# Gated attention and GLU on one core: loads of remixed input moved to SyncE, pair loads two periods later, routing sums in halves of 256 columns

## The chip, the cores and the metric

The kernel runs on one core of a Trainium2 chip. The metric is the device time of one execution in microseconds (us): the median of the runs shown. The engines are TensorE (PE), VectorE (DVE), ScalarE (ACT), GpSimd (POOL) and SyncE (SP); SP only issues transfers.

## What is computed

For 2048 tokens `x` of 512 columns, a gate chooses per token between two branches, a full softmax attention with 32 heads of 16 columns and a GLU with 1792 hidden columns, all in fp32:

```python
g = sigmoid((x * gate_w).sum(-1, keepdims=True))
qkv = x @ wqkv                                   # 32 heads, 16 columns each
p = softmax(q @ k.T * 16 ** -0.5)
a = (p @ v) @ wo
b = (sigmoid(x @ w_gate) * (x @ w_up)) @ w_down
out = g * a + (1 - g) * b
```

The sum in the first line, one number a token, is called the routing sum or logit here.

## The kernel before, in words

Products in fp32 are made from pairs of tiles, a rounded high part and what is left (`xh`, `xl` for the input). The attention runs in 256 steps of the loop `for k in range(NPER)`, here called periods: two heads by two key tiles at a time. A period has these parts.

- The scores of tiles that come later, on PE (line 709), and their exponentials on ACT (line 711), eight of 512 columns, into the tiles `p`.
- The scores of rows whose maxima are needed later, on PE (line 298), and their reductions on DVE (lines 311, 316, 318), nine in a period. Line 311 does one score tile in two parts of 192 and 320 columns, and begins DVE's work of the period. The maxima of a whole half of a pair of heads go through `mpad` and a transpose, every eighth period, into two rows of the tile `qs`, so that the exponentials need no subtraction.
- Twelve matmuls of the GLU and of the late projections (line 164, `dn`), which a generator `filling()` hands out as jobs `far`, `side` and `chain`; when such a sum is complete, `leave` (line 632) copies it with ACT into one of six `er` tiles, and POOL adds such tiles (line 567).
- At the end the values phase: 32 matmuls (line 874) of `p` with `v`. ACT copies the result in two halves (line 882, `sum` in the first period of a group of eight, else `part`), and POOL adds the `part` tiles (line 892).

The string `STEADY` fixes the order of words in a period, and PE, ACT, DVE and POOL execute in the order of the program (`ORDERED`). Only the order of the transfers on SP is chosen by the framework's scheduler.

`load_pair` (lines 258, 259) brings the next pair of heads, eight transfers into `qs` and `ks`, once in sixteen periods; the maxima's scores read it five periods later, since they run `LEAD` = 22 steps, eleven periods, ahead. `mixed_x` (line 401) replaces parts of `xh` and `xl` by sums and differences of input parts kept in `t_d`, at the ends of some jobs, 28 transfers in all. Between `k` = 75 and 122, in groups of six periods, `logit_load` brings 256 tokens (`xn`) and `logits` (line 859) makes two routing sums on DVE; in the same groups the late projections are split (`split_load`, `split_sum`).

Of the kernel before, what the change touches and what calls it, by code (L numbers as in the profile page):

```python
# [12 lines left out]
F32 = mybir.dt.float32  # L13
F32R = mybir.dt.float32r
AF = mybir.ActivationFunctionType
ALU = mybir.AluOpType
# [6 lines left out]
SYNC = mybir.DependencyInfo(mybir.DependencyClass.Sync, mybir.DependencyReason.DATA)  # L23

S, D, H, DH, F = 2048, 512, 32, 16, 1792
# [5 lines left out]
NPAIR = H // 2  # L31
# [16 lines left out]
def gated_mix(ctx, tc, x, xT, wqk, wv, wo, w_gate, w_up, w_down, gate_w, out):  # L48
    nc = tc.nc
    pe, act, dve, pool, sp = nc.tensor, nc.scalar, nc.vector, nc.gpsimd, nc.sync  # L50
# [6 lines left out]
    def turns(tiles):  # L57
        turn = iter(range(1 << 30))
        return lambda: tiles[next(turn) % len(tiles)]
# [18 lines left out]
    t_d = dram.tile([5, 2, 2, 2, P, 512], F32, name="t_d")  # L78
# [12 lines left out]
    logit = keep.tile([P, NS], F32, name="logit")  # L91
    g1 = keep.tile([P, NS], F32, name="g1")
    g0 = keep.tile([P, NS], F32, name="g0")
# [4 lines left out]
    def mid(name, dt=F32):  # L98
        return keep.tile([P, 4, 512], dt, name=name, tag="mid", bufs=3)
# [107 lines left out]
    gwb = xp.tile([P, D], F32, name="gwb")  # L207
# [189 lines left out]
    def mixed_x(n, c, k0, cx):  # L397

        cols = slice(cx * 512, (cx + 1) * 512)
        for a, xs in enumerate((xh, xl)):  # L400
            act.dma_start(xs[:, k0:k0 + 2, cols].bitcast(F32), t_d[n, a, c].rearrange("k p s -> p k s"))

    def o_and_r(u, ks, ot, rb):

# [224 lines left out]
                    kept_x(4, c, 2, c + 2)  # L629
        wd.extend(ws)  # L630

    leave = lambda e, o: act.activation(e, o, AF.Copy)
    fill = filling()


# [9 lines left out]
    for c in range(NC):  # L645
# [20 lines left out]
        for i, m in order:  # L666
            o, ops, dst = two[i]
# [23 lines left out]
        else:  # L691
            engine.tensor_copy(to, o)

    ptile = {}

    def st_part(k, b):

        p, r = divmod(2 * k, 32)
        i, kt = divmod(r, 16)
        qs, ks = QS[p % 2], KS[p % 2]  # L700
        r = 64 * b
        pt = ptile[k, b] = mid(f"p{k}_{b}")

        def steps():
            for a in range(2):
                for c in range(2):
                    o = bank()
                    q0 = i * 1024 + c * 512
                    pe.matmul(o, ks[r:r + KR, (kt + a) * P:(kt + a + 1) * P], qs[r:r + KR, q0:q0 + 512],  # L709
                              start=True, stop=True)  # L710
                    act.activation(pt[:, 2 * a + c, :], o, AF.Exp, scale=DH ** -0.5)  # L711
                    yield
        return steps()

# [136 lines left out]
    tok = {}  # L851
# [2 lines left out]
        tok[t] = keep.tile([P, 2, D], F32, name=f"xn{t}", tag="ev", bufs=2)  # L854
        sp.dma_start(tok[t], x[t * P:(t + 2) * P, :].rearrange("(t p) d -> p t d", p=P))

    def logits(t, a):
        xn = tok[t][:, a, :]
        dve.tensor_tensor_reduce(xn, xn, gwb, scale=1.0, scalar=0.0, op0=ALU.mult, op1=ALU.add,
                                 accum_out=logit[:, t + a:t + a + 1])  # L860

    VALUES = (("18", 0), ("19", 256))
    sums = {}
# [74 lines left out]
    bank = bankm = lambda: spot[0]  # L938
    for k in range(NPER):
        n = 2 * k  # L940
        if n + LEAD == NSTEP:
            last = [before[s] for s in ("14", "12", "17", "15", "18", "16", "19")]
            bank = turns(last)
            leave = dve.tensor_copy
        if 75 <= k < 123:
            t, r = divmod(k - 75, 6)
            if r in (0, 3):
                split_load(2 * t + r // 3)
            if r in (1, 4):
                split_sum(2 * t + r // 3)  # L950
            if r == 1:
                logit_load(2 * t)
            if r in (3, 4):
                logits(2 * t, r - 3)
        if n % 32 == 0 and n // 32 + 1 < NPAIR:
            load_pair(n // 32 + 1)
        parts["t0"], parts["t1"] = st_part(k, 0), st_part(k + 1, 1) if k + 1 < NPER else iter(())
        emit(STEADY if k < FREE else LAST, **parts)
        if run and run.done():
            run = next(fill, None)  # L960
        elif run and run.n:
            turn(run)
        for half in list(mrow):
            later[:0] = put_max(half)
        work(2.6)
        later.extend(soon)
        soon.clear()
        if k == NPER - 1:
            break
        if NPER - 16 < k <= NPER - 12:  # L970
            for _ in range(2):
                next(next(exps))
        if k < FREE:
            slots.update({"18": slots["10"], "19": slots["13"]})
        values(k)
        before, slots = slots, {}
        if k == NPER - 17:
            loaded.extend(hidden_load(*chunks[m]) for m in range(2))
            early = [hidden_early(m) for m in range(2)]
            exps = iter([early[0]] * 4 + [early[1]] * 4)  # L980
        if 192 <= k < 215 and k % 8 != 4:
            next(dens[0], None)
        if k == NPER - 6:
            next(dens[1])
        if k == NPER - 2:
            raws = [late_raw(*late[m][:2]) for m in range(2)]
        if k == NPER - 13:
            early = chain(*early)
        if k >= NPER - 13:
            for _ in range(1 if k < FREE else 3):  # L990
                next(early, None)
# [71 lines left out]
    at = dict(zip((9, 11, 13, 15, 18, 20, 23, 25), range(8)))  # L1063
# [66 lines left out]
```

## Time and profile before

| what | us |
|---|---|
| median of three runs (lowest, highest) | 1676.27 (1675.6, 1678.23) |
| the profiled execution | 1674.28 |
| its span | 1672.5 |
| PE busy | 1663.9 |
| DVE busy | 1470.0 |
| ACT busy | 1403.3 |
| POOL busy | 942.2 |

The span runs from the first to the last instruction of the profile. Busy time is summed over the whole span, while each stage has its own limits; the attention loop fills the time from 88 to 1486 us. A bracket behind a row of a timeline tells how long the engine was idle ahead of it and which event ended that.

### The profile page before, as it was taken

Reading aid. Unit: us, or ns where it says so; the run is one execution under the profiler, and the core shown is the slowest. Engines: PE = TensorE matmul, PEld = TensorE weight load, DVE = VectorE, ACT = ScalarE, POOL = GpSimd, SP = SyncE. Lnnn points to the kernel's source line nnn. Section 1 sums busy time; section 2 is a strip of 40 time slices with the busy share of each in tenths; the row PEclk is TensorE's granted clock in tenths of the full one; section 3 lists DMA queues with packets and bytes.
Section 4 is the critical chain, followed back from the end, with each engine's and each line's share of the span. In section 5 each row is a group of like instructions: output and inputs, shape, how many; then the busy total and the mean of one; then the engine's idle time right before and its main releaser. Section 6 shows DMA issues by size and latency. Waiting matters only on the chain.

```text
span 1672.5 us, 43216 instructions
## 1 busy us (share of the span) xinstructions
PE 1663.9 (99%) x16650; PEld 1211.0 (72%) x16650; DVE 1470.0 (88%) x2595; ACT 1403.3 (84%) x2901; POOL 942.2 (56%) x922
## 2 busy tenths in 40 slices
PE   9999999999999999999999999999999999999999
PEld 7777777777677777676677777777777777668887
DVE  7989999999889999999899999999999999886853
ACT  4189999999999999998899999999999999983431
POOL 1134576547656666566667677676766667553110
PEclk9999999999999999999999999999999999999999
DMA  8412447365555565556535353534353435368861
GB/s 271 121 47 62 131 170 214 139 186 191 152 192 153 159 165 162 148 160 197 138 110 141 109 147 103 141 103 135 111 134 109 134 115 171 110 214 267 300 211 70
DMA packets 143822, 254.75 MB, mean 152 GB/s; under 512 B 24256, under 2 KB 36544, under 8 KB 140736
## 3 DMA queue, kind: packets, MB, share of 16 engines
q1 hardware_dynamic: 135024, 235.34, 46.3%
q10 hardware_dynamic: 8592, 16.65, 3.2%
q8 instruction: 131, 2.15, 0.6%
q14 instruction: 75, 0.61, 0.1%
HBM read 149.42 MB, written 102.50 MB: 151 GB/s over the span
## 4 chain that ended last, share of the span: by engine, by line
PE 99%; DMA 1%; POOL 0%; DVE 0%; ACTq 0%; ACT 0%; issue 0%; SPq 0%; POOLq 0%
PE sm L874 21%; PE dn L164 17%; PE sm L709 13%; PE sm L298 10%; PE st L298 9%; PE st L874 7%; PE st L709 7%; PE st L1075 3%; PE sm L1075 3%; PE dn L1075 2%; PE st L164 2%; PE st L669 1%; PE sm L151 1%; PE st L151 1%; DMA qs<-q_d 0%; DMA side_7r<-in_w_up_dram 0%
## 5 line engine op out<-in xcount | busy, mean ns | idle before, releaser
L711 ACT ACTIVATE p<-sm 128x512 f32<-128x512 f32 x1274 | 704.0, 631 | 20.6 <-PE sm L709 10.4
L316 DVE TENSOR_REDUCE stat<-sm 128x1 f32<-128x512 f32 x802 | 521.3, 681 | 0.3 <-PE dn L164 0.2
L709 PE MATMUL sm<-qs,ks 64*128 64x512 f32 x1274 | 497.6, 417 | 0.0
L316 DVE TENSOR_REDUCE stat<-st 128x1 f32<-128x512 f32 x734 | 479.6, 681 | 4.2 <-PE dn L164 4.2
L711 ACT ACTIVATE p<-st 128x512 f32<-128x512 f32 x774 | 462.1, 636 | 9.4 <-PE st L709 0.3
L298 PE MATMUL sm<-ks,qs 48*128 48x512 f32 (+2 forms) x1192 | 421.8, 391 | 0.0
L298 PE MATMUL st<-ks,qs 48*128 48x320 f32 x1101 | 394.6, 390 | 0.0
L874 PE MATMUL sm<-p,v 128*17 128x256 f32 (+1 forms) x6000 | 377.6, 384 | 0.0
L892 POOL TENSOR_TENSOR sum<-sum,part 128x512 f32<-128x512 f32 x224 | 288.2, 1287 | 133.5 <-PE sm L709 34.9
L709 PE MATMUL st<-qs,ks 64*128 64x512 f32 x774 | 318.1, 427 | 3.7 <-ACT part L882 3.7
L874 PEld LDWEIGHTS sm<-p,v 128*17 128x17 f32 x6000 | 164.3, 97 | 159.1 <-DVE stat L316 32.1
L298 PEld LDWEIGHTS sm<-ks,qs 48*128 48x128 f32 x1192 | 200.5, 186 | 71.7 <-ACT part L882 49.6
L709 PEld LDWEIGHTS sm<-qs,ks 64*128 64x128 f32 x1274 | 233.3, 185 | 25.8 <-issue 5.1
L298 PEld LDWEIGHTS st<-ks,qs 48*128 48x128 f32 x1101 | 188.6, 186 | 66.0 <-ACT part L882 37.3
L567 POOL TENSOR_TENSOR chain<-chain,chain 128x512 f32<-128x512 f32 x96 | 124.3, 1295 | 150.6 <-PE sm L709 54.9
L882 ACT ACTIVATE part<-sm 128x256 f32<-128x256 f32 x306 | 125.9, 413 | 55.6 <-PE sm L874 54.3
L709 PEld LDWEIGHTS st<-qs,ks 64*128 64x128 f32 x774 | 142.5, 185 | 21.1 <-ACT part L882 4.6
L311 DVE TENSOR_REDUCE stat<-sm 128x1 f32<-128x192 f32 x245 | 97.6, 419 | 59.6 <-PE sm L298 58.8
L567 POOL TENSOR_TENSOR had<-chain,had 128x512 f32<-128x512 f32 x96 | 123.5, 1286 | 39.2 <-PE sm L709 19.7
L311 DVE TENSOR_REDUCE stat<-st 128x1 f32<-128x320 f32 x245 | 97.7, 420 | 47.5 <-PE st L298 47.0
L874 PE MATMUL st<-p,v 128*17 128x256 f32 (+1 forms) x2016 | 136.8, 389 | 0.0
L318 DVE TENSOR_REDUCE stat<-sm 128x2 f32<-128x512 f32 x145 | 97.9, 682 | 0.0
(917 smaller groups left out, 3590.8 us busy)
## 6 DMA issues: line engine op xcount, KB each, us to landing
gul<-gu_d SPq DMA_DIRECT2D x56, 512.0 KB
had<-gu_d SPq DMA_DIRECT2D x84, 256.0 KB
gu_d<-had SPq DMA_DIRECT2D x84, 256.0 KB
gu_d<-side SPq DMA_DIRECT2D x56, 256.0 KB
pv_d<-sum SPq DMA_DIRECT2D x32, 256.0 KB
qs<-q_d SPq DMA_DIRECT2D x30, 256.0 KB
ks<-k_d SPq DMA_DIRECT2D x30, 256.0 KB
gu_d<-far SPq DMA_DIRECT2D x28, 256.0 KB
```

The lines of the kernel that those rows point to most:

```text
L164: mm = pe.matmul(self.o, a[rows], b[rows], start=(self.n == 0), stop=(self.n == 2 * len(self.ops) - 1))
L298: pe.matmul(t[:, cols], qs[r:r + KM, qt * P:(qt + 1) * P], ks[r:r + KM, g * 512 + cols.start:g * 512 + cols.stop], start=True, stop=True)
L311: dve.tensor_reduce(to[:, a:a + 1], t[:, cols], axis=AX.X, op=ALU.max)
L316: dve.tensor_reduce(to[:, g + 1:g + 2], t, axis=AX.X, op=ALU.max)
L318: dve.tensor_reduce(to[:, :2], t.rearrange("p (a c) -> p a c", a=2), axis=AX.X, op=ALU.max)
L567: pool.tensor_tensor(to, u, w, ALU.add)
L709: pe.matmul(o, ks[r:r + KR, (kt + a) * P:(kt + a + 1) * P], qs[r:r + KR, q0:q0 + 512], start=True, stop=True)
L711: act.activation(pt[:, 2 * a + c, :], o, AF.Exp, scale=DH ** -0.5)
L874: pe.matmul(o[32 * c:32 * c + VW, cols], v[:, 2 * k % 16 + a, h * VW:(h + 1) * VW], pts[c // 2][:, 2 * a + c % 2, cols], start=(a == 0), s ...
L882: act.activation(e[:, cols], o[:, cols], AF.Copy)
L892: pool.tensor_tensor(s, s, e, ALU.add)
L1075: pe.matmul(down[t], a, b, start=(f == 0 and m == 0), stop=(f == NF - 2 and m == 5))
```

## The change

Four things are done. The loads of remixed input go out on SP's queue, not on ACT's. The load of the next pair of heads is written two periods later (`n % 32 == 4`). Each copy of `leave` is made to depend on the newest exponentials of the tiles that the coming ones replace, so that the first exponential of a period no longer names ACT's own earlier work in its wait. Each routing sum is made from two sums of 256 columns, the second of them into `g0`, which one addition joins to `logit` at `k` = 123; the four pieces for two tiles stand in four periods of a group of six, none in a period with the transposes (`k` % 8 == 4), and their load stands one period earlier.

```diff
@@ -398,7 +398,7 @@
 
         cols = slice(cx * 512, (cx + 1) * 512)
         for a, xs in enumerate((xh, xl)):
-            act.dma_start(xs[:, k0:k0 + 2, cols].bitcast(F32), t_d[n, a, c].rearrange("k p s -> p k s"))
+            sp.dma_start(xs[:, k0:k0 + 2, cols].bitcast(F32), t_d[n, a, c].rearrange("k p s -> p k s"))
 
     def o_and_r(u, ks, ot, rb):
 
@@ -629,7 +629,13 @@
                     kept_x(4, c, 2, c + 2)
         wd.extend(ws)
 
-    leave = lambda e, o: act.activation(e, o, AF.Copy)
+    def leave(e, o):
+        done = act.activation(e, o, AF.Copy)
+        for b in (0, 1):
+            if (at[0] - b, 1 - b) in exp_of:
+                tc.add_manual_dep(done.ins, exp_of[at[0] - b, 1 - b].ins.name, SYNC, reason="tiles of the next exponentials")
+
+    at = [0]
     fill = filling()
 
 
@@ -691,7 +697,7 @@
         else:
             engine.tensor_copy(to, o)
 
-    ptile = {}
+    ptile, exp_of = {}, {}
 
     def st_part(k, b):
 
@@ -708,7 +714,7 @@
                     q0 = i * 1024 + c * 512
                     pe.matmul(o, ks[r:r + KR, (kt + a) * P:(kt + a + 1) * P], qs[r:r + KR, q0:q0 + 512],
                               start=True, stop=True)
-                    act.activation(pt[:, 2 * a + c, :], o, AF.Exp, scale=DH ** -0.5)
+                    exp_of[k, b] = act.activation(pt[:, 2 * a + c, :], o, AF.Exp, scale=DH ** -0.5)
                     yield
         return steps()
 
@@ -854,10 +860,14 @@
         tok[t] = keep.tile([P, 2, D], F32, name=f"xn{t}", tag="ev", bufs=2)
         sp.dma_start(tok[t], x[t * P:(t + 2) * P, :].rearrange("(t p) d -> p t d", p=P))
 
-    def logits(t, a):
-        xn = tok[t][:, a, :]
-        dve.tensor_tensor_reduce(xn, xn, gwb, scale=1.0, scalar=0.0, op0=ALU.mult, op1=ALU.add,
-                                 accum_out=logit[:, t + a:t + a + 1])
+    def logits(t):
+
+        for a in range(2):
+            for to, cols in ((logit, slice(0, D // 2)), (g0, slice(D // 2, D))):
+                xn = tok[t][:, a, cols]
+                dve.tensor_tensor_reduce(xn, xn, gwb[:, cols], scale=1.0, scalar=0.0, op0=ALU.mult, op1=ALU.add,
+                                         accum_out=to[:, t + a:t + a + 1])
+                yield
 
     VALUES = (("18", 0), ("19", 256))
     sums = {}
@@ -938,6 +948,7 @@
     bank = bankm = lambda: spot[0]
     for k in range(NPER):
         n = 2 * k
+        at[0] = k
         if n + LEAD == NSTEP:
             last = [before[s] for s in ("14", "12", "17", "15", "18", "16", "19")]
             bank = turns(last)
@@ -948,11 +959,16 @@
                 split_load(2 * t + r // 3)
             if r in (1, 4):
                 split_sum(2 * t + r // 3)
-            if r == 1:
+            if r == 0:
                 logit_load(2 * t)
-            if r in (3, 4):
-                logits(2 * t, r - 3)
-        if n % 32 == 0 and n // 32 + 1 < NPAIR:
+                pieces = logits(2 * t)
+                busy = [a for a in range(6) if (k + a) % 8 == 4]
+                free = [a for a in range(1, 6) if a not in busy][-4:]
+            if r in free:
+                next(pieces)
+        if k == 123:
+            dve.tensor_tensor(logit, logit, g0, ALU.add)
+        if n % 32 == 4 and n // 32 + 1 < NPAIR:
             load_pair(n // 32 + 1)
         parts["t0"], parts["t1"] = st_part(k, 0), st_part(k + 1, 1) if k + 1 < NPER else iter(())
         emit(STEADY if k < FREE else LAST, **parts)
```

PE and POOL have the same instructions in the same order as before. Three places show what moves on the others. The names: `side16_10` is an `er` tile of a `side` job, `part126` the values of period 126, `p127_0` the exponentials of period 127; `_49` in a wait stands for a value of the semaphore, and `Activation` is ACT itself.

ACT at the end of period 126, before:

```order
L632 ACTIVATE side16_10_11073<-dn_68 128x512 [waits DMAHW0_49,PE_49]
L401 DMA xh_107<-t_d_79 128x2x512 [waits DMAHW1_49]
L401 DMA xl_108<-t_d_79 128x2x512 [waits DMAHW2_49]
L882 ACTIVATE part126_11097<-st0_65 128x256 [waits DVE_49,PE_49,Pool_49]
L882 ACTIVATE part126_11097<-sm0_69 128x256 [waits PE_49]
L711 ACTIVATE p127_0_11100<-st2_67 128x512 [waits PE_49,Activation_49]
L711 ACTIVATE p127_0_11100<-st0_65 128x512 [waits PE_49]
L711 ACTIVATE p127_0_11100<-sm0_69 128x512 [waits PE_49]
```

and after:

```order
L633 ACTIVATE side16_10_11090<-dn_68 128x512 [waits DMAHW0_49,PE_49,Activation_49]
L892 ACTIVATE part126_11114<-st0_65 128x256 [waits DVE_49,PE_49,Pool_49]
L892 ACTIVATE part126_11114<-sm0_69 128x256 [waits PE_49]
L717 ACTIVATE p127_0_11117<-st2_67 128x512 [waits PE_49]
L717 ACTIVATE p127_0_11117<-st0_65 128x512 [waits PE_49]
L717 ACTIVATE p127_0_11117<-sm0_69 128x512 [waits PE_49]
```

The two transfers are gone, the first exponential waits for PE alone, and the wait on ACT stands at the copy `side16_10`.

SP around the load of the pair at `k` = 128, before:

```order
L569 DMA gu_d_75<-side16_01_10995 128x512 [waits Pool_49]
L110 DMA chain1_0r_11156<-in_w_up_dram 128x512 [waits DMAHW6_49]
L110 DMA chain1_7r_11158<-in_w_up_dram 128x512 [waits DMAHW7_49,Pool_49]
L258 DMA qs1_102<-q_d_73 32x1x2048 [waits DMAHW0_49,PE_49]
L528 DMA gu_d_75<-side16_10_11073 128x512 [waits DMAHW3_49,Activation_49]
L259 DMA qs1_102<-q_d_73 16x2048 [waits DMAHW4_49]
L258 DMA qs1_102<-q_d_73 32x1x2048 [waits DMAHW5_49,PE_49]
L259 DMA qs1_102<-q_d_73 16x2048 [waits DMAHW6_49]
L258 DMA ks1_103<-k_d_74 32x1x2048 [waits DMAHW1_49]
L259 DMA ks1_103<-k_d_74 16x2048 [waits DMAHW2_49]
L258 DMA ks1_103<-k_d_74 32x1x2048 [waits DMAHW3_49]
L259 DMA ks1_103<-k_d_74 16x2048 [waits DMAHW4_49]
```

and after:

```order
L401 DMA xh_107<-t_d_79 128x2x512 [waits DMAHW1_49,PE_49]
L401 DMA xl_108<-t_d_79 128x2x512 [waits DMAHW2_49]
L110 DMA chain1_0r_11173<-in_w_up_dram 128x512 [waits DMAHW3_49]
L110 DMA chain1_7r_11175<-in_w_up_dram 128x512 [waits DMAHW4_49,Pool_49]
L258 DMA qs1_102<-q_d_73 32x1x2048 [waits DMAHW5_49]
L569 DMA gu_d_75<-side16_11_11167 128x512 [waits DMAHW6_49,Pool_49]
L904 DMA pv_d_76<-sum7_1_10637 128x512 [waits DMAHW7_49,Pool_49]
L259 DMA qs1_102<-q_d_73 16x2048 [waits DMAHW0_49]
L258 DMA qs1_102<-q_d_73 32x1x2048 [waits DMAHW1_49]
L569 DMA gu_d_75<-had00_00_11171 128x512 [waits DMAHW2_49,Pool_49]
L259 DMA qs1_102<-q_d_73 16x2048 [waits DMAHW3_49]
L258 DMA ks1_103<-k_d_74 32x1x2048 [waits DMAHW4_49]
```

The loads `xh` and `xl` of ACT's queue stand here now, and rows that wait for POOL stand between the transfers of the pair, whose last ones follow three rows further on.

DVE at the first routing sum of the tokens `xn4`, before (the row without a wait reads the accumulator):

```order
L316 TENSOR_REDUCE stat6_0_7735<-st2_67 128x1 [waits PE_49]
L316 TENSOR_REDUCE stat6_0_7735<-st1_66 128x1 [waits PE_49]
L859 ISA xn4_7967,logit_96<-xn4_7967,gwb_109 128x512 [waits DMAHW3_49,DMAHW4_49,DMAHW1_49,DMAHW5_49,DMAHW0_49,Pool_49]
L859 ISA logit_96 128x1
L311 TENSOR_REDUCE stat6_0_7735<-sm3_72 128x1 [waits PE_49]
```

and after:

```order
L316 TENSOR_REDUCE stat6_0_7738<-sm1_70 128x1 [waits PE_49]
L316 TENSOR_REDUCE stat6_0_7738<-st1_66 128x1 [waits PE_49]
L868 ISA xn4_7895,logit_96<-xn4_7895,gwb_109 128x256 [waits DMAHW4_49,DMAHW3_49,DMAHW7_49,DMAHW0_49,Pool_49]
L868 ISA logit_96 128x1
L311 TENSOR_REDUCE stat6_0_7738<-sm3_72 128x1 [waits PE_49]
```

The instruction has 256 columns in place of 512. On SP its load `xn4` stands so before:

```order
L847 DMA q_d_73<-sq3_7642 128x512 [waits DMAHW1_49,Pool_49]
L569 DMA gu_d_75<-side11_01_7785 128x512 [waits Pool_49]
L528 DMA gu_d_75<-side11_10_7864 128x512 [waits DMAHW3_49,Activation_49]
L110 DMA side1_2r_7944<-in_w_up_dram 128x512 [waits DMAHW4_49,Pool_49]
L855 DMA xn4_7967<-in_x_dram 128x2x512 [waits DMAHW5_49,DMAHW1_49,DMAHW0_49]
```

and after:

```order
L853 DMA q_d_73<-sq3_7646 128x512 [waits DMAHW0_49,Pool_49]
L569 DMA gu_d_75<-side11_01_7788 128x512 [waits DMAHW1_49,Pool_49]
L528 DMA gu_d_75<-side11_10_7868 128x512 [waits Activation_49]
L845 DMA sq4_7893<-s_d_80 128x512 [waits DMAHW3_49,DVE_49]
L861 DMA xn4_7895<-in_x_dram 128x2x512 [waits DMAHW7_49,DMAHW4_49,DMAHW0_49]
```

It has come ahead of the weight load `side1_2r`, and the load `sq4`, which stood above these rows, right ahead of it.

## Rows read from the trace of the kernel before

**Rows 1.** The page's chain of work that ended last, shares by engine.

```profile
PE 99%; DMA 1%; POOL 0%; DVE 0%; ACTq 0%; ACT 0%; issue 0%; SPq 0%; POOLq 0%
```

**Rows 2.** Stretches: length, PE, PEld, DVE, ACT, POOL busy, PE clock, DMA share, GB/s.

```profile
352.75:440.86 88.11, 88.11 (x981) 63.79 (x984) 79.92 (x149) 82.73 (x177) 54.05 (x55) 1.00 0.57 175
440.86:530.17 89.31, 88.92 (x980) 63.34 (x984) 81.22 (x153) 82.83 (x177) 56.61 (x60) 1.00 0.55 169
530.17:618.90 88.73, 88.73 (x980) 63.16 (x984) 82.91 (x159) 83.11 (x177) 56.43 (x65) 1.00 0.59 168
618.90:708.21 89.31, 89.31 (x980) 63.09 (x984) 83.41 (x159) 83.36 (x177) 57.02 (x65) 1.00 0.54 160
708.21:802.38 94.17, 90.82 (x980) 63.76 (x984) 83.45 (x158) 83.15 (x177) 56.74 (x63) 0.98 0.63 182
```

**Rows 3.** Timeline of ACT: start, length, what, idle ahead and releaser; quiet period.

```profile
604.29 0.39 ACT L882 ACTIVATE part<-sm 128x256 f32<-128x256 f32 x1 [0.25 <-PE sm L874]
604.75 0.60 ACT L711 ACTIVATE p<-st 128x512 f32<-128x512 f32 x1
```

**Rows 4.** Timeline of DVE, the first reductions of the same period.

```profile
604.54 0.76 DVE L311 TENSOR_REDUCE stat<-sm 128x1 f32<-128x192 f32 x2 [0.56 <-PE sm L298]
```

**Rows 5.** Timeline of ACT, a first exponential that came late.

```profile
443.52 1.58 ACT L711 ACTIVATE p<-sm 128x512 f32<-128x512 f32 x3 [0.35 <-PE st L298]
```

**Rows 6.** Chain in order of time, 440 to 820: start, length, what.

```profile
446.62 1.85 PE sm L874 x32
...
464.02 1.85 PE sm L874 x32
...
524.66 0.99 PE st L874 x16
...
780.28 1.85 PE sm L874 x32
786.22 1.00 PE st L874 x16
...
789.35 7.56 DMA qs<-q_d
802.38 1.85 PE sm L874 x32
```

**Rows 7.** Timeline of DVE, two reciprocals one period apart.

```profile
1228.05 0.54 DVE L830 RECIPROCAL den<-den 32x64 f32<-32x64 f32 x1
...
1233.59 0.55 DVE L830 RECIPROCAL den<-den 32x64 f32<-32x64 f32 x1
```

**Rows 8.** Timeline of ACT, copies of the values behind loads of line 401.

```profile
460.36 0.39 ACT L882 ACTIVATE part<-st 128x256 f32<-128x256 f32 x1 [1.34 <-DVE stat L311]
...
797.41 0.38 ACT L882 ACTIVATE part<-st 128x256 f32<-128x256 f32 x1 [4.29 <-DMA qs<-q_d]
```

**Rows 9.** Timeline of SP's queue: last load of a pair, load of x.

```profile
531.50 0.58 SPq L259 DMA_DIRECT2D ks<-k_d  x1
...
566.52 0.38 SPq L855 DMA_DIRECT2D xn<-in_x_dram  x1
```

**Rows 10.** Line 711: semaphore events, ns min/median/max, first and last start.

```profile
L711 ACTq EVENT_SEMAPHORE  x254: 17/17/17, 90.7 to 1482.9; - x127
```

**Rows 11.** Line 859: the routing sums, ns min/median/max, first and last start.

```profile
L859 DVE CUSTOM_DVE_ANT_0 xn<-xn,gwb x16: 649/682/1285, 515.1 to 754.0; 128x512 f32<-128x512 f32 x16
```

**Rows 12.** The page's groups: busy us, mean ns, idle before, releaser.

```profile
L311 DVE TENSOR_REDUCE stat<-sm 128x1 f32<-128x192 f32 x245 | 97.6, 419 | 59.6 <-PE sm L298 58.8
```

**Rows 13.** Timeline of DVE, the longest routing sum.

```profile
647.97 1.28 DVE L859 CUSTOM_DVE_ANT_0 xn<-xn,gwb 128x512 f32<-128x512 f32 x1
```

**Rows 14.** Timeline of POOL at the same time.

```profile
647.98 0.73 POOL L473 TENSOR_TENSOR side_11r<-side_11r 128x256 f32<-128x256 f32 x1
```

**Rows 15.** DMA engines, 566 to 571: busy tenths in 40 slices.

```profile
DMA  8999500000001699999959989899981100009016
```

**Rows 16.** SP's queue, 560 to 575, who waited for whom: total, times, longest.

```profile
SPq L569 <- POOL side L567: 7.1, 2, 4.4
```

## The prediction

> **What bounds the kernel now.** I read the chain that ended last first: TensorE (PE) is 99% of it [rows 1]. That doesn't make the matmuls the bound, because a PE that is fed late also counts as busy. So the second view is the busy time in stretches of sixteen periods of the attention loop (a period is one pass of `k`, from one values phase to the next). A stretch with nothing odd in it takes 88.11 us, 5.507 us a period; the four stretches behind it take 89.31, 88.73, 89.31 and 94.17 [rows 2], together 9.08 us more than four quiet ones. The change touches these four stretches and, by one wait, every period. So I ask two questions: what sets 5.507, and where the 9.08 went.
>
> In a quiet period ScalarE (ACT) ends its second copy of the values at 604.68 and starts the first exponential .07 us later [rows 3]; VectorE (DVE) idles .56 us ahead of its first reduction, for PE to bring the first scores [rows 4]. Behind these starts both engines run without idling until the next values phase. Both chains are needed by the matmuls of the period, and both have hardly any slack. For ACT: in one period the first exponential started .35 us behind the copy instead of .07 [rows 5], and that period took 5.76 (440.86, the start in [rows 2], to 446.62 [rows 6]), .25 over 5.507. Of .28 late, .25 came out at the end: ACT's slack is some .03 at most. For DVE: a reciprocal of .54 us set into the gap of .56 makes the period 5.54 long (1228.05 to 1233.59 [rows 7]), .03 more. DVE's slack is about nothing.
>
> The 9.08 by the chain in order of time: 446.62 to 464.02 is 17.40 for three periods, .88 over; 780.28 to 786.22 is 5.94, .43 over; 786.22 to 802.38 is 16.16 for two, 5.15 over [rows 6]. In each of the three, ACT's stream has the loads of remixed input (line 401) between the `leave` copy and the copies of the values: ahead of the first copy at 460.36 ACT idles 1.34 us, and ahead of the one at 797.41 it idles 4.29, ended by the transfer `qs<-q_d` [rows 8]. The ACT queue waited for a DMA lane still held by a pair load, which took 7.56 us to land [rows 6]. Together 6.46. Two periods with a late first exponential, whose cause I don't see, make .5 (the one above and one like it). What is left of the 9.08, 2.1 us, sits in periods with a logit sum on DVE (line 859).
>
> **The change part by part.**
>
> Loads of remixed input on SyncE (SP). 28 issues leave ACT, and with them the three stalls: a gain of 6.46. The other 22 issues stood where they delayed nothing, and give nothing back. On SP each costs an issue of about .38 us, as a load of x does [rows 9], and a wait for PE or a lane; behind them on SP are stores of `side` and `had` tiles and weight loads. The tiles that they write are read by the following job of sums, at least three periods (16.5 us) on; the longest landing that the chain shows is 7.56. I cost this at nothing. If a store behind them were held for so long that the ring of six `er` tiles ran out, ACT's `leave` would wait, as it does for nothing now. Bounds of this part: a gain between 5.5 (a third of the smaller stalls comes back) and 7.
>
> Later pair loads (two periods, 11.0 us). Nothing is removed from an engine; the eight transfers only stand clear of the period in which the last stall was. The first reader of a new pair is the maxima's matmul five periods after the old issue. Take the pair of `k` = 80: this period starts when the values phase of 524.66 [rows 6] has ended, at 526.5, and five periods (27.5) on, at 554.0, the maxima need the pair. The last `ks` was issued at 531.50 [rows 9]; with the longest landing, 7.56, it was there at 539.1. So 14.9 us were to spare, and with 11.0 less it is 3.9. This slack hides the move, and I cost it at nothing; what it costs if the slack is gone is the third rival.
>
> First exponential with one wait. 254 of these held a second semaphore event of 17 ns [rows 10]; 236 lose it, and the wait on ACT's older exponentials moves to the `leave` copies, where it has long been fulfilled. The exponential can start earlier by at most the .07 that ACT idles ahead of it: .07 by 236 is 16.5 us as the upper end; the lower end is 0, because an earlier exponential makes nothing late. I take the low side: the reciprocal's row says that DVE, untouched by this, repeats every 5.507 by itself, and its slack is the same to about a hundredth. So .005 (0 to .015) by 236, 1.2 us (0 to 3.5).
>
> Logit sums in halves. A whole one takes .68 at the median, 1.285 at the most [rows 11]. Most whole ones cost their period next to nothing, though they are longer than the gap of .56: neighbouring DVE instructions overlap, so the gap takes .68. A half reads 256 columns; the reductions of 192 and of 320 columns take .42 in the mean [rows 12], which leaves .26 of room. Moving them out of the periods with the transposes of the maxima takes away another cause of lateness. So most of the 2.1 goes. What stays: the longest one, at 647.97, [rows 13] started together with a POOL addition that ran to 648.71 [rows 14], and was .60 longer than the median. If one in sixteen meets such a one, two of 32 halves do, each .60 − .26 = .34 late: .7 stays. The gain is 1.4 (0 to 2.1). The joining addition on DVE is 16 columns, less than the .42 of a half, once, in a period without a sum: nothing, at most .4.
>
> The Trainium skill, "SBUF — State Buffer", section "Who interferes with whom", has a rule that speaks against this part: DVE and GpSimd share one port pair, locked for a whole instruction, and a DVE instruction with two SBUF inputs is blocked by a GpSimd one that reads SBUF. The row at 647.97 agrees (the .73 of POOL's instruction and some .55 behind it make the 1.28). By it the halving doubles the number of chances to be blocked; the second rival gives the time of that.
>
> Loads of x. In four of the eight groups the first half is now read one period behind the load, not two. In the group of [rows 9] the load was issued at 566.52, and the DMA engines are busy to about 569.9 [rows 15], so it lands near 570. The changed order puts it behind one store and one load, near 565.9 by my estimate; the piece's gap is at 570.7. It fits by about .9. Cost nothing; the first rival is that it doesn't.
>
> Sum: 6.46 + 1.2 + 1.4 = 9.1 us. The profiled execution took 1674.28; it would be 1665.2. That run lies 2.0 below the median of 1676.27, so I forecast 1667.2 for the median. Worst to best of the bounds: gains of 5.5 to 12.6, 1670.8 to 1663.7.
>
> **The rivals.**
>
> First, late loads of x. Their landing then is that of crowded stretches, up to 7.56 [rows 6] instead of 4: 565.9 + 7.56 is 573.5, 2.8 after the gap, and DVE's reductions queue behind the waiting half. In four groups that costs up to 11 us, with landings of 6 us about 5. The time is 1672 to 1678. For it: the queue of SP now holds more. Against: only four groups, and a landing of 4 in the row.
>
> Second, blocked halves. If every third of 32 halves starts under a POOL addition of 1.28 and waits for nearly all of it, ten cost 1.28 − .26 = 1.0 each: 10 us, and the gain is gone, 1677. Against: one of sixteen whole ones was hit so hard.
>
> Third, slower: late pair loads. Their spare time is 3.9. In the new SP order stores that wait for POOL stand among the eight transfers; such a wait was up to 4.4 us in one stretch of 15 us [rows 16]. Where these waits together pass 3.9 the maxima's matmuls wait for the pair, PE stands still, and ACT and DVE behind it. If that makes 5 us, about as the last stall (5.15), and happens with three of the fifteen pairs, the time is 1667.2 + 15 = 1682. It decides from a delay of 3.9 on. Against it: such a wait holds one row of SP, and the other pairs' landings may be shorter than 7.56.
>
> Fourth, faster: ACT alone sets the period, and DVE's rows are read wrongly. Then the full .055 (.07 less what a single wait needs) by 236 is 13.0 instead of 1.2: 1655.4. Against it stands the reciprocal's row.
>
> That the change doesn't do what it says is small: the order shows ACT without the loads, and the exponentials with one wait.
>
> **How the numbers follow.** Forecast .66; first rival .12, second .06, third .10, fourth .06. A measurement of this kernel tells about 0.2%, 3.4 us: faster is under 1672.9, slower over 1679.6. Faster: .66 + .06 + .06 (half of the first rival) is .78; same: the other half of the first, the second, is .12; slower: .10. The range has the forecast's whole range, the first rival's nearer part and a part of the optimism about the first exponential: 1662 to 1675, which leaves out the third and the fourth rival and a piece of the second.
>
> **What would show it.** ACT's stream has no DMA rows, and no idle over .4 ahead of the values' copies in 440 to 810. The four stretches of [rows 2] take 88.1 to 88.6 each. A quiet period is 5.50 (5.507 now); at 5.45 the fourth rival is right. The halves take .35 to .45, a blocked one is seen by its length. A wait of DVE for a transfer ahead of a half is the first rival; a PE idle ahead of line 298 in the fifth period after a pair's loads, with a lower granted clock, is the third. I am wrong by a step if the stalls of ACT only move to PE at the jobs' ends, because the loads on SP land too late for the sums.

## The result and the profile after

The changed kernel takes 1680.2 us in the median (before 1675.44 over the same comparisons), a ratio of 1.0026 with an interval of 1.0019 to 1.0033. I had forecast 1667.2 in a range of 1662 to 1675. The ratio is taken without one slow run of the kernel before. So it is slower by 0.26%, outside the range, and on the side to which I had given 1 in 10.

The chain of the profile after, which answers to [rows 1], has transfers at 2%, where they were 1%:

```profile
PE 97%; DMA 2%; SPq 0%; DVE 0%; POOL 0%; ACTq 0%; issue 0%; ACT 0%; POOLq 0%; DVEq 0%
```

The stretches of sixteen periods of the changed kernel, with the columns of [rows 2]; the first is a quiet one, the following ones answer to the rows there, and the last is the one behind:

```profile
266.86:355.03 88.17, 88.17 (x978) 64.09 (x976) 79.88 (x149) 83.30 (x177) 51.35 (x59) 1.00 0.49 157
355.03:444.70 89.67, 88.44 (x978) 63.62 (x977) 79.98 (x149) 83.42 (x177) 53.89 (x55) 1.00 0.56 177
444.70:533.44 88.74, 88.74 (x978) 63.56 (x976) 81.39 (x157) 83.54 (x177) 55.51 (x59) 1.00 0.52 164
533.44:623.57 90.13, 90.13 (x979) 62.01 (x977) 85.27 (x169) 84.13 (x177) 56.54 (x66) 1.00 0.59 170
623.57:714.25 90.68, 90.49 (x979) 62.46 (x977) 85.31 (x171) 84.13 (x177) 57.10 (x65) 1.00 0.53 157
714.25:802.71 88.46, 88.46 (x977) 63.37 (x976) 82.94 (x164) 83.26 (x177) 55.30 (x63) 1.00 0.56 174
802.71:896.41 93.70, 90.04 (x979) 64.38 (x977) 79.97 (x149) 83.57 (x177) 60.75 (x57) 0.98 0.43 131
```

The 94.17 of before have fallen to 88.46, as forecast. But 93.70 stands one stretch later, 89.67 where there was nothing, and the two stretches with routing sums have grown to 90.13 and 90.68.

From the starts of the values phases I took the length of every period in both profiles, the mean of the undisturbed ones, and what the others are over it. Periods are counted from the first values phase as 0, so period 127 is the one with the 4.29 us of [rows 8]. The two profiled executions stand 5.9 us apart (1674.28 and 1680.14):

| where | before | after | difference |
|---|---|---|---|
| time to the first values phase | 88.33 | 90.46 | +2.1 |
| an undisturbed period, mean (the difference is for 243) | 5.5071 | 5.5098 | +0.7 |
| periods 67, 125, 127 (ACT's copies behind line 401) | 6.45 | 0 | −6.45 |
| periods 56, 128, 129 | 0 | 7.17 | +7.2 |
| periods with routing sums | 2.06 | 5.40 | +3.3 |
| periods 64, 119 (late first exponential) | 0.52 | 0 | −0.5 |
| time from the last values phase on | 185.98 | 185.61 | −0.4 |

The first row is no part of the change, nor is the last: the order of all engines up to the first period is the same in both but for a wait, and the other kernels below, which also leave that stage alone, start their first values phase anywhere from 88.1 to 90.0, and the time from the last values phase on is 185.6 to 186.4 in them. Of what is left, the three stalls went as I had said and came back in two other places, and the routing sums became later and not earlier.

The larger of the new stalls, in order of time along the chain of the changed kernel (start, length, what):

```profile
797.74 0.76 SPq L401
...
798.56 0.76 SPq L110
...
799.41 9.49 DMA chain_7r<-in_w_up_dram
...
809.04 0.73 POOL chain_0r L473
...
809.84 0.72 POOL chain_7r L473
...
810.67 0.78 PE dn L164
```

And PE's timeline there:

```profile
806.61 0.40 PE L298 MATMUL st<-ks,qs 48*128 48x512 f32 x1
810.67 0.78 PE L164 MATMUL dn<-xh,cb(0, 0)h 64*128 64x512 f32 x1 [3.66 <-POOLq L175]
```

The weights of the coming job (`chain_0r`, `chain_7r`) are issued behind the loads of line 401 and take 9.49 us to land. POOL has reached the first addition that reads them (line 473) and waits. PE doesn't need these weights yet: it waits for line 175, the empty instruction on POOL with which `turn` hands a bank from one half of PE to the other, and that stands behind POOL's waiting one. PE stands still for 3.66 us, and its matmuls then run slower for a while (.78 and then .62 for .40). The granted clock, the last but two of the columns, is 1.00 ahead of the pause and .52 behind it, that is from the higher of the clock's two levels (2.4 GHz) to about the lower (1.2 GHz):

```profile
797.00:803.00 6.00, 6.00 (x72) 4.16 (x73) 5.43 (x11) 5.69 (x14) 1.82 (x2) 1.00 0.98 348
810.60:814.00 3.40, 3.33 (x19) 2.08 (x23) 1.19 (x2) 1.82 (x4) 3.28 (x4) 0.52 0.19 70
```

Pause and slow matmuls together make the 5.29 of period 128 and the .28 of the next.

### The profile page after: what moved, and what is told of

It is laid out like the page before. It is cut to its first block, busy times and chain, and to the rows that moved or that the text cites. A ratio compares the mean times of both kernels' runs of the same rounds, so it can differ in the third digit from the quotient of the medians.

```text
span 1678.3 us, 43152 instructions
## 1 busy us (share of the span) xinstructions
PE 1666.8 (99%) x16650; PEld 1208.6 (72%) x16650; DVE 1474.0 (88%) x2628; ACT 1411.4 (84%) x2901; POOL 939.6 (56%) x922
## 4 chain that ended last, share of the span: by engine, by line
PE 97%; DMA 2%; SPq 0%; DVE 0%; POOL 0%; ACTq 0%; issue 0%; ACT 0%; POOLq 0%; DVEq 0%
PE sm L884 20%; PE dn L164 16%; PE sm L715 13%; PE sm L298 10%; PE st L298 10%; PE st L884 7%; PE st L715 7%; PE st L1091 3%; PE sm L1091 3%; PE dn L1091 2%; PE st L164 2%; PE sm L151 1%; PE st L675 1%; PE st L151 1%; DMA chain_7r<-in_w_up_dram 1%; DMA chain_3r<-in_wqk_dram 0%
```

## The experiments

**One part at a time.** Four kernels carry one part of the change each, on the kernel before.

```diff
-            act.dma_start(xs[:, k0:k0 + 2, cols].bitcast(F32), t_d[n, a, c].rearrange("k p s -> p k s"))
+            sp.dma_start(xs[:, k0:k0 + 2, cols].bitcast(F32), t_d[n, a, c].rearrange("k p s -> p k s"))
```

> The kernel before with one part of the change alone: the loads of remixed input on SyncE. Theory Q (they stand ahead of the next job's weights on SyncE's queue, so the weights land late and PE waits for them at line 164): the three stalls of ACT in the periods 67, 126 and 127 (0.88, 0.43, 5.15 us) are gone, but two new ones stand at the starts of the two chain stages, 1 to 2 us at about 400 us and 4 to 6 us in period 128; in sum within 0.15% of before (1673 to 1678). Theory P (the stall of period 128 comes from the later pair loads): no period over 6.1 us between 440 and 810 us, and 6 us less than before (about 1669.5).

Ratio 1.0017 (1.0006 to 1.0028). Periods 67, 125 and 127 are clean; 56 is 3.80 over, 128 and 129 are 5.32 and 1.23 over. PE's timeline shows the same wait at both places:

```profile
404.91 0.79 PE L164 MATMUL dn<-xh,cb(2, 0)h 64*128 64x512 f32 x1 [2.12 <-POOLq L175]
...
808.94 0.79 PE L164 MATMUL dn<-xh,cb(0, 0)h 64*128 64x512 f32 x1 [3.66 <-POOLq L175]
```

Theory Q holds: this part alone makes both stalls, with the pair loads where they were. The one at 56 is larger than the 1 to 2 us that I expected and than the 1.58 of the changed kernel (the weights took 8.13 us to land there, in the changed kernel 7.23), and the time, 1679.05, is just past the range. (What the expectation calls period 126 is 125 in this count.)

The second kernel has the dependence of `leave` on the exponentials, and nothing else.

> The kernel before with one part alone: the first exponential without its second wait. Theory D (DVE's chain sets the quiet period as much as ACT's): the first exponential starts 0.06 us earlier behind PE's restart (0.54 for 0.60), a quiet period stays within 0.005 us of 5.507, the time within 0.1% of before. Theory A (ACT sets the period): 5.45 a period and some 13 us less.

Ratio 0.9993 (0.9985 to 1.0002). The first exponential starts .54 us behind PE's restart for .60, and a quiet period is 5.5096, .0025 longer than before. So theory A falls. The two periods of .25 with a late first exponential are gone here and in the changed kernel; with the second wait they come at changing places (two before, five in the kernel with the later pair loads alone, none in the first). What makes them is not shown.

The third has the halves, their places and their loads.

> The kernel before with one part alone: routing sums in halves, their places and their earlier loads. Theory H (halves are late for three reasons: locked out by POOL, standing right behind the transposes of the maxima, waiting for their load of x): the excess of the periods with such sums rises from 2.1 to between 4 and 6 us, so 2 to 4 us slower than before (0.1 to 0.25%). Rival (the lateness in the changed kernel came with SyncE's fuller queue): the excess is under 2.1 us, and the time is that of before or 1 us less.

Ratio 1.0071 (1.0058 to 1.0083), 12 us slower. Besides what was expected of H (4.6 us in eleven periods) period 81 is 9.87 over:

```profile
547.46 0.43 DVE L862 CUSTOM_DVE_ANT_0 xn<-xn,gwb 128x256 f32<-128x256 f32 x1 [8.82 <-issue]
```

The profile names no releaser here. The load of `xn` stands on SP behind the eight transfers of the pair of `k` = 80; it was issued at 540.74 in this run, 6.7 us ahead of the half. Theory H has waits for x, but none of this size.

The fourth has the later pair loads.

```diff
-        if n % 32 == 0 and n // 32 + 1 < NPAIR:
+        if n % 32 == 4 and n // 32 + 1 < NPAIR:
```

> The kernel before with one part alone: pair loads two periods later, the loads of remixed input still on ACT. Theory Q: the stall of ACT in period 127 hung on the lane that a pair load held; with the pair's transfers issued later or not, the loads of line 401 still wait on ACT for lanes, so between 0 and 5 us less than before (1670.5 to 1676). Theory P: a stall of 4 to 6 us in period 128 or 129 on PE, for pair transfers beside the weights of the chain stage, and no gain in the total.

Ratio 1.001 (1.0001 to 1.0019). ACT's stall stays, 6.55 over in period 127:

```profile
796.75 0.38 ACT L882 ACTIVATE part<-st 128x256 f32<-128x256 f32 x1 [4.75 <-DMA qs<-q_d]
```

The transfer that it waits for was issued at 788.36, where before it was 789.35 [rows 6]: two periods later in the program is not later on SP, whose queue runs ahead of the program's periods. Theory P falls, and of the 0 to 5 us that theory Q left open nothing was gained: 127 is 1.4 longer than before, 67 and 125 together 0.97 shorter. What this part is for shows with the halves:

> The kernel before with the halves and the later pair loads. Theory X (the halves' load of x is late by 9.9 us in period 81 since it stands behind the eight transfers of a pair; the later pair loads are what brings it in time): the stall of period 81 falls under 1 us, ACT's stall of 5 to 6 us in period 127 stays, 1676 to 1680. Rival: the 9.9 us stay, since the scheduler puts the pair's transfers where it likes.

Ratio 1.002 (1.0011 to 1.0029): period 81 falls from 9.87 to 0.10 over, 127 stays at 5.97. The load of `xn` is issued at 533.98. So later pair loads bring the load of x in time, about 9.8 us, which the halves alone had lost.

**The order on SP.** The remixed input goes out on SP, and the loads of the second column half are put behind the next weights. Their readers are the seventh and eighth sums of the stage.

```diff
-                            mixed_x(1 + a, c, 2 * a, c + 2)
+                            if c == 0:
+                                mixed_x(1 + a, c, 2 * a, c + 2)
+                            else:
+                                put_off.append((1 + a, c, 2 * a, c + 2))
...
+                if kind == "chain" and at == 2:
+                    while put_off:
+                        mixed_x(*put_off.pop(0), behind=newest[0])
```

`newest` holds the last load of weights; each deferred load is made to depend on it.

> The loads of remixed input on SyncE as in the change, nothing else of it, but those of the second column half (two of four pairs of loads at each of the two job ends) are written two sums into the chain stage, behind the weights of the chain's second job. Theory Q (the stalls at 400 us and in period 128 come from POOL waiting for these weights, which land behind the remixed input, with the token that PE waits for behind POOL's waiting instruction): both stalls fall to under 1 us together, ACT's three stalls stay away, 5 to 6.5 us less than before (1669 to 1671). Rival B (the transfers of these stages are more than the DMA engines can move in the time, in whatever order): a stall of 3 to 6 us stays in periods 127 to 131, and the time is within 2 us of before.

1668.86 us, ratio 0.996 (0.9947 to 0.9974). The stalls of ACT and those of PE are gone. The stretches that were 88.11 and 94.17 before, and the one behind:

```profile
353.03:441.13 88.10, 88.10 (x979) 63.60 (x977) 79.92 (x149) 82.84 (x177) 54.07 (x55) 1.00 0.57 175
...
707.33:795.63 88.30, 88.30 (x979) 63.59 (x977) 82.39 (x157) 82.85 (x177) 56.16 (x63) 1.00 0.60 166
795.63:883.72 88.09, 88.09 (x978) 63.82 (x977) 79.92 (x149) 82.85 (x177) 61.03 (x57) 1.00 0.49 147
```

The same bytes are moved by the same engines, so rival B falls: it was the order and the moment of issue, not capacity. The weights of the larger stall show what changed. On SP's timeline, before, in the changed kernel and in this one, and POOL's first addition of these weights in this one:

```profile
788.91 0.33 SPq L110 DMA_DIRECT2D chain_7r<-in_w_up_dram  x1
```

```profile
799.41 0.43 SPq L110 DMA_DIRECT2D chain_7r<-in_w_up_dram  x1
```

```profile
788.49 1.10 SPq L113 DMA_DIRECT2D chain_7r<-in_w_up_dram  x1
```

```profile
797.05 0.73 POOL L478 TENSOR_TENSOR chain_0r<-chain_0r,chain_7r 128x256 f32<-128x256 f32 x1 [0.41 <-DMA chain_7r<-in_w_up_dram]
```

Period 127 starts at 791.67, 797.20 and 790.13 in the three. So the weights were issued 2.8 us ahead of it before, 2.2 behind it in the changed kernel and 1.6 ahead of it here. They still took some 8.4 us to land here, and POOL waited .41 for them, without harm. Against this kernel the changed one loses 3.8 us by the issue, behind loads that waited on SP for PE (up to 1.6 us for one), and 1.1 by the landing: the place in the queue is the larger part. The same edit on the whole changed kernel:

> The changed kernel whole, with the remixed input of the second half written behind the weights as in e5. Theory Q: the stalls of periods 56 and 128 (1.6, 5.3 and 0.3) go, the lateness of the routing sums (5.4) stays, and the time is 6 to 7.5 us less than the changed kernel: 1672 to 1674, 2 to 4 us less than before. Rival: in the changed kernel the pair's loads stand among these rows, so that a stall of 2 us or more stays near period 128.

1669.12 us, ratio 0.9965 (0.9951 to 0.9979), some 10 us less than the changed kernel and more than I expected: the stalls at 56, 128 and 129 are gone, and of the 5.4 us in periods with routing sums 4.0 stay. That is 8.6 of the 10; the rest does not stand in these periods.

**The routing sums.** On the changed kernel, with the product left out:

```diff
-                dve.tensor_tensor_reduce(xn, xn, gwb[:, cols], scale=1.0, scalar=0.0, op0=ALU.mult, op1=ALU.add,
-                                         accum_out=to[:, t + a:t + a + 1])
+                dve.tensor_reduce(to[:, t + a:t + a + 1], xn, axis=AX.X, op=ALU.add)
```

> The changed kernel, each half routing sum replaced by a plain sum of the 256 columns without the product with gate_w, so that DVE's instruction reads one SBUF tile and not two (the routing sums then lack gate_w). Theory L (a half with two SBUF inputs is locked out while POOL reads SBUF): no half takes over 0.45 us, and the lateness of periods 82, 88, 101, 106, 112 (2.4 us) goes; that of periods 76, 81, 84, 87, 100, 108 and 111 (transposes ahead, or a wait for the load of x; 2.8 us) stays. Rival (halves are long for some other reason, their landing or DVE itself): halves over 0.8 us stay.

In the changed kernel (ns, minimum, median, maximum) and then in this one, where the halves stand in two groups, for `logit` and for `g0`:

```profile
L868 DVE CUSTOM_DVE_ANT_0 xn<-xn,gwb x32: 382/416/1550, 513.3 to 765.7; 128x256 f32<-128x256 f32 x32
```

```profile
L868 DVE TENSOR_REDUCE logit<-xn x16: 376/408/421, 511.5 to 755.6; 128x1 f32<-128x256 f32 x16
L868 DVE TENSOR_REDUCE g<-xn x16: 407/410/414, 516.6 to 761.1; 128x1 f32<-128x256 f32 x16
```

No half is long when it reads one tile, though POOL starts an operation of 1.28 or 1.29 us within .01 of it in periods 82, 88 and 106. (The edit takes away the second input and also the written tile; that it is the input the run alone does not show.) Lateness in the periods with sums falls from 5.40 to 2.25, in the one run of this kernel. What goes is that of 82, 88, 101, 106, 109 and 112 (2.5 us), that of 81, a wait that this run didn't have, most of that of 87, a shorter wait here, and .37 of the .59 of 76; what stays is .22 or .23 each in 76, 84, 100 and 108 (transposes ahead) and 1.28 in 111 (a wait for x). The longest one of the changed kernel beside POOL shows the mechanism; first DVE, then POOL:

```profile
680.64 1.55 DVE L868 CUSTOM_DVE_ANT_0 xn<-xn,gwb 128x256 f32<-128x256 f32 x1
```

```profile
680.62 1.29 POOL L138 TENSOR_TENSOR sq<-sq 128x512 fp32r<-128x512 f32 x1
```

DVE's half started .02 us behind POOL's, waited for all of it, and ended .28 after it. And in period 84 the half stands right behind the transpose:

```profile
558.29 0.21 DVE L324 STREAM_TRANSPOSE mt<-mpad 128x32 f32<-128x32 f32 x1
558.43 0.38 DVE L868 CUSTOM_DVE_ANT_0 xn<-xn,gwb 128x256 f32<-128x256 f32 x1
```

Then the two whole sums that stand right behind the transposes, on the kernel with the weights first:

```diff
-            if r in (3, 4):
-                logits(2 * t, r - 3)
+            spots = (3, 5) if (k - r + 4) % 8 == 5 else (3, 4)
+            if r in spots:
+                logits(2 * t, spots.index(r))
```

(The expectation calls the kernel with the weights first e5.)

> The kernel with the remixed input behind the weights (e5), and the two whole routing sums that stand right behind the transposes of the maxima (periods 84 and 108 of the list) moved one period on. Theory H: these two periods lose their 0.45 us each, and nothing else changes: 0.5 to 0.9 us less than e5, about 1668. Rival (the moved sums meet POOL's work or wait instead): no gain over e5.

1667.51 us, ratio 0.9953 (0.9941 to 0.9966), the fastest version that computes everything. Period 84 is clean (0.45 before the move); the sum moved from 108 to 109 is .54 late there, and period 128 is .45 over, which it isn't with the weights first alone. Its gain over the kernel with the weights first is within the intervals, and I call it not shown.

**What sets a quiet period.** The earlier exponential had gained nothing. First I shortened DVE's work, a reduction of the tile with the last of four key groups:

```diff
-                    dve.tensor_reduce(to[:, g + 1:g + 2], t, axis=AX.X, op=ALU.max)
+                    some = t[:, :256] if g == 3 and b == 0 else t
+                    dve.tensor_reduce(to[:, g + 1:g + 2], some, axis=AX.X, op=ALU.max)
```

> The kernel before, one of the nine reductions of each period over 256 columns and not 512 (the maxima leave out these columns), which shortens DVE's work of a period by about 0.27 us. Theory D (DVE and ACT set the period together, with slack of hundredths on either): a quiet period falls by 0.01 to 0.03, no more, since ACT holds it: 2 to 7 us less than before. Rival (ACT has more slack): it falls by 0.1 or more.

> The kernel before with the same shorter reduction and with the first exponential's second wait taken away. Theory D: now that DVE has slack, the exponential that starts 0.06 us earlier shortens the quiet period by 0.04 to 0.06 against the run with the shorter reduction alone, 9 to 14 us less. Rival (the early exponential helps nobody, since later exponentials wait for PE's scores): the same quiet period as in that run.

Ratios 0.9987 (0.9978 to 0.9996) and 0.9986 (0.9977 to 0.9995); the quiet periods are 5.5082 and 5.5102. Neither moved, so theory D as I had written it falls, or the reduction was the wrong one. The routing sums are some 1.3 us less late in both; that this is the small gain is not shown. Next, two shorter score tiles on PE and DVE:

> The kernel before with two of the score tiles of each period (one in each row half of PE) computed and reduced over 256 columns and not 512; the maxima leave out these columns. It takes one eighth of a microsecond or less from PE's stream in a period, and 0.27 from DVE's. Theory T (PE's own stream of loads and matmuls sets 5.507; ACT and DVE come just in time): the quiet period falls by 0.05 to 0.11, 12 to 25 us less. Theory D' (some other chain through ACT sets it): it stays within 0.02 of 5.507, as with the shorter reduction alone.

Ratio 0.9951 (0.9937 to 0.9964), a quiet period of 5.4868. That is .02 less, short of what T asked and at the edge of D'. (It makes 4.9 of the 8 us by the ratio; the routing sums, which are not late here, make 2.) To see why I laid the starts of PE's thirty weight loads of a period, from its restart, beside the ends of ACT's and DVE's instructions (medians of the quiet periods). Two loads stand right behind such an end: that of the last maxima's scores at 2.995, .053 behind the end of DVE's fifth reduction (2.942), and that of the last scores at 3.205, .05 behind the end of ACT's fifth exponential (3.155). One period of the kernel before, restarted at 310.47, first PE's weight loads, then DVE's fifth reduction, which ends at 313.42:

```profile
313.47 0.18 PEld L298 LDWEIGHTS st<-ks,qs 48*128 48x128 f32 x1
313.68 0.18 PEld L709 LDWEIGHTS sm<-qs,ks 64*128 64x128 f32 x1
```

```profile
312.74 0.68 DVE L316 TENSOR_REDUCE stat<-st 128x1 f32<-128x512 f32 x1
```

I had shortened the sixth reduction, which comes too late to matter. So the edit was repeated with `g == 2`, the fifth, with and without the second wait of the exponential:

> The kernel before with the same fifth reduction over 256 columns alone. Theory T2: the weights that waited for DVE start earlier, those that wait for ACT stay at 3.206 us behind PE's restart, so the quiet period falls by about 0.02, to 5.485 to 5.50, 2 to 6 us less. Rival (ACT holds nothing): 5.47 or less already here.

> The kernel before without the first exponential's second wait, and with the fifth reduction of each period over 256 columns and not 512 (the maxima leave out these columns). Theory T2 (two waits hold the end of PE's stream, .01 to .02 us apart in effect: the last maxima's weights wait for the end of DVE's fifth reduction, the last scores' weights for the end of ACT's fifth exponential): with both brought forward the quiet period falls to 5.44 to 5.47, 9 to 16 us less than before. Rival (neither chain; PE's stream is full anyway): 5.49 or more.

| kernel | quiet period | last maxima's load | last scores' load | values |
|---|---|---|---|---|
| before | 5.507 | 2.995 | 3.205 | 3.656 |
| earlier exponential alone | 5.510 | 2.995 | 3.176 | 3.659 |
| shorter fifth reduction alone | 5.487 | 2.825 | 3.204 | 3.635 |
| both | 5.460 | 2.796 | 3.177 | 3.606 |

The ratios are 0.9964 (0.9953 to 0.9975) and 0.991 (0.9894 to 0.9927). The weight loads of a period with the shorter fifth reduction alone now name the engine that is left:

```profile
312.71 0.18 PEld L710 LDWEIGHTS sm<-qs,ks 64*128 64x128 f32 x1 [0.20 <-ACT p L712]
```

Theory T2 holds: two waits hold the end of PE's stream, one on DVE and one on ACT, and a wait taken from one of them shows in full only when the other is brought forward too. The fifth reduction alone gives .020 us a period, the exponential's earlier start alone nothing, both .047. With the fifth reduction short, the earlier start is worth .027 us a period, 6.6 us in 243. The medians of the two kernels, 1670.41 and 1660.61, are further apart; what makes the rest is not shown.

## Why the prediction was wrong

The loads of remixed input. That ACT's three stalls would go, and their size of 6.46, was right. The step that failed is the one behind it: "I cost this at nothing". I looked at who reads the loaded tiles, three periods on, and named the weight loads behind them on SP, but took no look at who waits for those. The rows of SP in the section on the change show `xh`, `xl` and then `chain1_0r`, `chain1_7r`. The loads wait there for PE, which reads the tiles that they overwrite, and the weights behind them were issued 5.0 us later against the period than before. The price of a burst stood in [rows 6], 7.56 us for one landing; with the remixed input ahead the weights took 9.49 (some 8.4 with its second half behind them). The wait then goes through POOL, which executes in order, to an empty instruction that PE needs. The term was −6.46 and measured +0.7 (−6.45 and +7.17). My own last sentence in the prediction had a stall moved to PE at the jobs' ends, for another reason (the remixed input itself late), and I gave it no chance of its own.

The routing sums. −1.4 was forecast, with 0 as the worst; it measured +3.3. Three steps failed. "Moving them out of the periods with the transposes" was read from the code, `k` % 8 == 4, without a look at where the transposes stand: they are the last work of that period on DVE, so the piece that is written in the following one stands right behind them. The changed kernel has four such pieces (76, 84, 100, 108; 1.2 us, of which the run with one input keeps 0.9), before there were two. The lockout by POOL I had as the second rival, but took two meetings in 32 for the forecast; six cost 2.5 us, up to 1.1 above the median. The rule of the Trainium skill, "SBUF — State Buffer", section "Who interferes with whom", agrees with the run with one input (.376 to .421 us) and with the row at 680.64 (1.55 us). That halves meet more such chances the prediction had worked out from it, and gave it too little weight. Waits for x were the first rival, at .12: they came in three groups (81, 87, 111) and cost 1.6, where I had put 5 to 11. (At 111 the profile names a load of weights that was issued right behind that of x as what came last; in the run with one input it names x.)

The later pair loads. That they delay no reader held: none of the stalls is a wait of PE for a pair, and the third rival, slower by late pairs, was not the mechanism. What I missed is their worth, 9.8 us beside the halves.

The first exponential. The mechanism was right, that DVE's chain leaves nothing for it; the size was off, +.0025 a period for −.005, and the place was shown only by the runs: not DVE's first reduction but its fifth. The fourth rival, at 1655.4, fell: its .055 a period from ACT alone were not there, and with DVE's fifth reduction shortened too it was .047.

So between the 9.1 us to gain and the 4.8 lost by the medians lie 13.9: 7.2 are the loads' term, 4.7 the sums', and 1.4 the exponential's (0.2 lost, as 0.7 in quiet periods less 0.5 for the two late ones, where 1.2 were to be won). The 0.6 that is left is less than runs of one kernel differ by.

## What to carry to other kernels

A transfer that is moved to another queue must be costed by everything that stands behind it there, down to the engine that waits, and that engine's own queue: here PE waited for an instruction that does nothing, because its neighbour on POOL waited for data. Where several engines come just in time, look for the instruction of the bound engine that waits last on each of them, and shorten the work that ends there; here work taken away behind that point gave nothing, and one of two such waits alone gave nothing or less than half of both. A period that is named in the code is not the place where its last instruction runs.

## What the runs showed of the hardware

A first exponential that waits for one semaphore started .54 us behind PE's restart in a quiet period, one that waits for two at .60. A routing half of 256 columns took .38 to .43 us where no POOL instruction under way held it, and up to 1.55 beside POOL; a reduction over one tile of the same size took .376 to .421 in all 32 cases, in the same places. Eleven halves of the changed kernel began .02 to .58 us behind a POOL instruction, and each ended .28 us behind that one's end, however long it was; eight whole sums of the kernel before ended .55 or .56 behind theirs. A pause of PE of 3.66 us was followed by a granted clock of .52 (810.60 to 814.00), one of 1.23 us at period 56 by one of 1.00 (404 to 407).
